# Where the first dense layer's gate is computed: m(2t - m) with three passes on VectorE in place of max, add and min over VectorE and GpSimd

## The chip, the cores and the metric

The kernel runs on one core of a Trainium2 chip. A core has five engines with queues of their own: TensorE (PE, matrix products and transposes), VectorE (DVE), ScalarE (ACT), GpSimd (POOL) and SyncE (SP, which here issues the DMAs). Each works through its queue in order; between engines, semaphores say when an input is there. The metric is the time of one execution on the device, in microseconds (us), lower being better.

## The reference

An attention over 4 batches, 8 heads, 1152 positions and 64 columns, whose queries are averaged in pairs (576 queries remain), then two dense layers over the resulting 2304 rows of 512 columns. The gate that the change concerns is `g`:

```python
h = x @ w_in                                   # 2304 x 2048
g = np.where(h >= 1, h, np.where(h <= -1, 0.0, (h + 1) ** 2 / 4))
x = g @ w_out                                  # 2304 x 512
h = np.maximum(np.maximum(x @ w1, x @ w2), x @ w3)
out = h @ w_o2
```

With t = relu(h/2 + 1/2), the gate is 0 where t is 0, t squared where t is up to 1, and 2t - 1 above. Both the old and the new formula give that.

## The kernel before

The attention runs in 48 units: batch b, a block i of 192 queries, and a pair p of heads. Each unit computes three blocks of scores (line 352, 128 x 1152, "sc"). For each block DVE takes the row maximum (line 366, "st"), ScalarE turns it into a bias (367) and takes the exponentials (368, "pf"). For two of three blocks, in batches 1 to 3, ScalarE then makes a half-precision copy (421), DVE subtracts it to get the rest (422, "hl"), and a DMA transposes both. The third block is transposed by TensorE (404), copied by ScalarE (410) and its rest is taken by DVE (411). The product with the values is line 440 ("av"), scaled by DVE in line 453 ("xf") and, every fourth unit, split into two half-precision parts (245 on GpSimd, 246 on DVE). The same pair of lines splits queries, keys and values. Queries come by DMA and are added in pairs by GpSimd in line 321 ("qn"). The next batch's keys and values are prepared in four units around a change of batch.

The first dense layer follows the attention by six units: from then on each unit also holds two tiles of the "up" product (line 506, 48 products of 192 columns) and one block of the "down" product (line 532). An up tile is 128 x 384 and goes through lines 511 to 517: ScalarE makes t (511, tile "t2", "t" in the profile), three operations make the gate in place with a second tile "rl", GpSimd makes its half-precision part (515) and DVE the rest (517). Both are inputs of line 532. There are 96 such tiles. Twelve come after the last unit, in a tail in which the second layer's weights are prepared as well (lines 155 to 161, 147, 148, 664 to 675). One of the four weight blocks there is split on GpSimd, in lines 672 and 673. The second layer (lines 752 to 785) comes last.

The order on TensorE is written out by hand for the attention (`ORDER`); on the other engines, and in the tail on TensorE too, a scheduler puts the instructions in order when the program is built, from its own estimate of their durations. A change of a few operations can so move others. "t2" and "rl" have two buffers each.

Of the kernel before, what the change touches and what calls it, by code (L numbers as in the profile page):

```python
# [12 lines left out]
ALU = mybir.AluOpType  # L13
# [38 lines left out]
def body(ctx: ExitStack, tc: tile.TileContext, q, k, v, w_in, w_out, w1, w2, w3, w_o2, out):  # L52
    nc = tc.nc
# [416 lines left out]
    def scales(b):  # L470
        hu = small.tile([P, 1], F32, tag="hu", name=f"hu{b}")
        hh = small.tile([P, 1], F32, tag="hh", name=f"hh{b}")
        nc.vector.tensor_scalar(out=hu, in0=U_in[:, 1:2], scalar1=Uv[b][:, NPAIR:NPAIR + 1],
                                scalar2=None, op0=ALU.mult)
        nc.vector.tensor_scalar(out=hh, in0=Uv[b][:, NPAIR + 1:NPAIR + 2], scalar1=0.5, scalar2=None, op0=ALU.mult)

        gd = small.tile([P, 1], F32, tag="dgd", name=f"dgd{b}")
        gs = small.tile([P, 1], F32, tag="dgs", name=f"dgs{b}")
        nc.vector.tensor_scalar(out=gd, in0=hu, scalar1=2.0 ** 31, scalar2=1.0, op0=ALU.mult, op1=ALU.max)
        nc.vector.tensor_scalar(out=gd, in0=gd, scalar1=2.0 ** -15, scalar2=None, op0=ALU.mult)  # L480
        nc.vector.reciprocal(out=gs, in_=gd)
        dst[b] = hh, gd, gs
# [3 lines left out]
    def acc(x, name):  # L486
        ps, tag = room[x]
        return ps.tile([P, 512], F32, tag=tag, name=name)

    def up_steps(b, i):  # L490

        if i == 0:
            scales(b)
        hh, gd, gs = dst[b]
        x = xh.pop((b, i))
        g = gp.tile([P, 2, NF, NB], F16, tag="g", name=f"g{b}_{i}")
        gt[b, i] = g
        for f2 in range(NF // 2):
            key = f"{b}_{i}_{f2}"
            fs = slice(2 * f2, 2 * f2 + 2)  # L500
            ph = acc("h", "ph" + key)[:, :2 * NB].rearrange("p (a n) -> p a n", a=2)
            for a in range(2):
                ff = 2 * f2 + a
                for kt in range(KD):
                    for e, (wi, xi) in enumerate(((0, 0), (0, 1), (1, 0))):
                        nc.tensor.matmul(ph[:, a], win[:, wi, kt, ff * P:(ff + 1) * P], x[:, xi, kt],  # L506
                                         start=(kt == 0 and e == 0), stop=(kt == KD - 1 and e == 2))

            t2 = room["t2"].tile([P, 2, NB], F32, tag="t2", bufs=room["n"], name=f"t2_{key}")
            rl = room["t2"].tile([P, 2, NB], F32, tag="rl", bufs=room["n"], name=f"rl_{key}")  # L510
            nc.scalar.activation(out=t2, in_=ph, func=AF.Relu, scale=hh, bias=0.5)
            nc.vector.tensor_scalar(out=rl, in0=t2, scalar1=1.0, scalar2=-1.0, op0=ALU.max, op1=ALU.add)  # L512
            nc.gpsimd.tensor_tensor(out=rl, in0=t2, in1=rl, op=ALU.add)  # L513
            nc.vector.scalar_tensor_tensor(out=t2, in0=t2, scalar=1.0, in1=rl, op0=ALU.min, op1=ALU.mult)  # L514
            nc.gpsimd.tensor_scalar(out=g[:, 0, fs, :], in0=t2, scalar1=gs, scalar2=1.0,  # L515
                                    op0=ALU.mult, op1=ALU.mult)
            nc.vector.scalar_tensor_tensor(out=g[:, 1, fs, :], in0=t2, scalar=gs, in1=g[:, 0, fs, :],  # L517
                                           op0=ALU.mult, op1=ALU.subtract)
            yield
# [20 lines left out]
    def dense_steps(units):  # L540

        down = iter(())
        for b, i in units:
            for k, _ in enumerate(up_steps(b, i)):
                yield
                if k % 2 == 1:
                    next(down, None)
                    yield
                    yield
            down = down_steps(b, i)  # L550
        for _ in down:
            yield
            yield
# [299 lines left out]
```

## Time and profile before

| | before |
|---|---|
| median of 2 runs | 1233.24 us (1231.83 to 1234.66) |
| the profiled execution | 1239.84 us, span on the core 1237.9 us |
| PE busy | 1077.9 us (87%) |
| DVE busy | 857.5 us (69%), 1454 instructions |
| ACT busy | 696.8 us (56%) |
| POOL busy | 302.9 us (24%), 306 instructions |
| mean granted TensorE clock | 0.958 of full speed |

Line numbers are those of the kernel before. Times within the trace count from the start of the span. In a timeline a row says when an instruction began, how long it took, and in brackets how long its engine was idle before and what ended that. Instructions of one engine overlap by a little at their edges. The shares in the table are means over stages that have different limits, so stages and waits are read one by one.

### The profile page before, as it was taken

The numbers are of one execution on the slowest core, as the hardware profiler recorded it, in microseconds if no ns is written. First come the engines' busy times: TensorE is split into PE (matmuls) and PEld (weight loads), VectorE is DVE, ScalarE is ACT, GpSimd is POOL, SyncE is SP. The second block draws the span as 40 slices with busy tenths as digits, with TensorE's granted clock in tenths as the row PEclk, the third lists the DMA queues.
The fourth block names the chain that finished last, engine by engine and source line by source line (L and its number), as shares of the span: only waits on it lengthen the run. The fifth ranks groups of instructions, "written<-read, shape, count | busy, mean of one in ns | idle before, by whom it ended". The sixth has DMA issues, their size and how long they took to land.

```text
span 1237.9 us, 26735 instructions
## 1 busy us (share of the span) xinstructions
PE 1077.9 (87%) x11058; PEld 881.2 (71%) x11058; DVE 857.5 (69%) x1454; ACT 696.8 (56%) x1241; POOL 302.9 (24%) x306
## 2 busy tenths in 40 slices
PE   0456788899999987999988899998697999999998
PEld 0334567677788876888877788887696876767774
DVE  3988765657888888988888988886988652322220
ACT  3868676656667777667776677766453411122111
POOL 1310012323222344322234422221643020100000
PEclk9867889999999999999999999999899999999999
DMA  9963211446766688965588766547433220000001
GB/s 289 267 199 106 90 27 26 84 87 155 129 113 120 109 172 170 167 110 110 110 158 177 146 105 107 97 88 157 160 96 117 90 67 18 10 27 18 17 18 43
DMA packets 273753, 134.90 MB, mean 109 GB/s; under 512 B 229088, under 2 KB 256736, under 8 KB 272608
## 3 DMA queue, kind: packets, MB, share of 16 engines
q1 hardware_dynamic: 273632, 133.20, 48.5%
q8 instruction: 86, 1.41, 0.5%
q14 instruction: 35, 0.29, 0.1%
HBM read 62.39 MB, written 9.44 MB: 58 GB/s over the span
## 4 chain that ended last, share of the span: by engine, by line
PE 41%; DVE 17%; issue 7%; DMA 7%; ACT 6%; POOL 4%; SPq 2%; ACTq 0%; POOLq 0%; DVEq 0%
PE p L752 17%; PE po L769 5%; PE ph L506 5%; PE py L532 4%; DVE st L366 4%; DMA qn<-in_q_dram 3%; PE sc L352 3%; PE tr L404 3%; PE av L440 2%; DVE g L517 2%; DVE hl L422 2%; DVE t L514 2%; ACT pf L368 1%; POOL g L515 1%; ACT hl L421 1%
## 5 line engine op out<-in xcount | busy, mean ns | idle before, releaser
L352 PE MATMUL sc<-kst,qst 128*64 128x512 f16 (+3 forms) x1152 | 178.2, 347 | 62.6 <-DMA qst<-qpre 21.1
L532 PE MATMUL py<-g,wou 128*128 128x192 f16 x2304 | 201.1, 248 | 22.4 <-POOL g L515 7.8
L752 PE MATMUL p<-yh,wm 128*128 128x288 f16 x1728 | 216.0, 287 | 3.7 <-ACT py L536 2.7
L532 PEld LDWEIGHTS <-wou 128*128 128x128 f16 x2304 | 191.3, 99 | 31.8 <-issue 31.4
L506 PE MATMUL ph<-xh,win 128*128 128x192 f16 x2304 | 203.2, 249 | 4.9 <-ACT py L536 2.6
L366 DVE TENSOR_REDUCE st<-sc 128x1 f32<-128x1152 f32 x144 | 194.1, 1348 | 18.0 <-PE sc L352 17.8
L752 PEld LDWEIGHTS <-wm 128*128 128x128 f16 x1728 | 169.6, 98 | 49.6 <-issue 4.4
L506 PEld LDWEIGHTS <-win 128*128 128x128 f16 x2304 | 195.1, 99 | 7.5 <-issue 5.7
L368 ACT ACTIVATE pf<-sc,st,esc 128x1152 f32<-128x1152 f32 x144 | 188.7, 1311 | 4.5
L352 PEld LDWEIGHTS <-qst 128*64 128x64 f16 (+1 forms) x1152 | 85.6, 109 | 124.3 <-issue 56.9
L513 POOL TENSOR_TENSOR rl<-t,rl 128x384 f32<-128x384 f32 x96 | 103.7, 1083 | 185.3 <-DVE rl L512 185.3
L404 PE MATMUL tr<-ident,pf 128*128 128x128 f32 x648 | 98.9, 306 | 26.3 <-ACT pf L368 17.4
L422 DVE TENSOR_TENSOR hl<-pf,hl 128x1152 f16<-128x1152 f32 x72 | 104.3, 1449 | 22.7 <-ACT hl L421 22.6
L404 PEld LDWEIGHTS tr<-ident,pf 128*128 128x128 f32 x648 | 83.5, 161 | 40.9 <-ACT pf L368 24.8
L367 ACT ACTIVATE st<-st,esc 128x1 f32<-128x1 f32 x144 | 41.6, 289 | 119.0 <-DVE st L366 118.8
L760 ACT ACTIVATE h<-mx 128x288 f16<-128x288 f32 x48 | 21.2, 442 | 133.3 <-DVE mx L758 133.3
L757 DVE TENSOR_TENSOR mx<-p,mx 128x288 f32<-128x288 f32 x48 | 21.9, 456 | 106.3 <-PE p L752 105.7
L515 POOL TENSOR_SCALAR g<-t,dgs 128x384 f16<-128x384 f32 x96 | 70.7, 738 | 97.0 <-DVE t L514 91.4
L440 PE MATMUL av<-pt,vhl 128*64 128x192 f16 x1944 | 87.1, 247 | 2.7 <-DMA pt<-hl 2.7
L440 PEld LDWEIGHTS <-vhl 128*64 128x64 f16 x1944 | 79.3, 110 | 12.4 <-issue 8.5
L517 DVE SCALAR_TENSOR_TENSOR g<-t,dgs,g 128x384 f16<-128x384 f32 x96 | 74.2, 781 | 16.4 <-POOL g L515 16.2
L421 ACT ACTIVATE hl<-pf 128x1152 f16<-128x1152 f32 x72 | 83.4, 1159 | 0.9
(169 smaller groups left out, 1339.0 us busy)
## 6 DMA issues: line engine op xcount, KB each, us to landing
kn<-in_k_dram SPq DMA_DIRECT2D x16, 576.0 KB, 4.6
vn<-in_v_dram SPq DMA_DIRECT2D x16, 576.0 KB, 5.0
raw_m<-in_moe_w_dram SPq DMA_DIRECT2D x12, 768.0 KB, 5.1
raw_in<-in_moe_w_in_dram SPq DMA_DIRECT2D x8, 1024.0 KB, 5.4
qn<-in_q_dram SPq DMA_DIRECT2D x24, 256.0 KB, 4.0
raw_ou<-in_moe_w_out_dram SPq DMA_DIRECT2D x10, 512.0 KB, 4.6
qst<-qst SPq DMA_DIRECT2D x48, 96.0 KB, 2.2
y_d<-ys SPq DMA_DIRECT2D x48, 96.0 KB, 2.0
```

Of the source, the lines that this page charges most:

```text
L352: nc.tensor.matmul(sc[m0:m1, n0:n1], qst[b, i, p][who][:, var, m0:m1], ks[:, h, n0:n1], start=(var == 0), stop=(var == 1))
L366: nc.vector.tensor_reduce(out=m, in_=sc, axis=AX.X, op=ALU.max, negate=True)
L368: nc.scalar.activation(out=pf, in_=sc, func=AF.Exp, bias=nb, scale=e, accum_out=sums[b, i, p][:, who:who + 1])
L404: nc.tensor.transpose(tr[:, c * P:(c + 1) * P], pf[:, c * P:(c + 1) * P], ident)
L421: nc.scalar.activation(out=hl[:, 0], in_=pf, func=AF.Copy)
L422: nc.vector.tensor_tensor(out=hl[:, 1], in0=pf, in1=hl[:, 0], op=ALU.subtract)
L440: nc.tensor.matmul(acc[64 * h:64 * h + 64], vhl[b, p][:, vi, h, c, :], pt[:, h, pi * KT + c, :], start=(c == 0 and e == 0), stop=(c == KT ...
L506: nc.tensor.matmul(ph[:, a], win[:, wi, kt, ff * P:(ff + 1) * P], x[:, xi, kt], start=(kt == 0 and e == 0), stop=(kt == KD - 1 and e == 2))
L513: nc.gpsimd.tensor_tensor(out=rl, in0=t2, in1=rl, op=ALU.add)
L517: nc.vector.scalar_tensor_tensor(out=g[:, 1, fs, :], in0=t2, scalar=gs, in1=g[:, 0, fs, :], op0=ALU.mult, op1=ALU.subtract)
L532: nc.tensor.matmul(py, wou[:, ff // 2, wi, ff % 2, m * P:(m + 1) * P], g[:, gi, ff, :], start=(ff == 0 and e == 0), stop=(ff == NF - 1 and ...
L752: nc.tensor.matmul(ph[:, :NB2], wm[:, wi, i, kt, ff * P:(ff + 1) * P], yh[:, yi, kt, n0:n0 + NB2], start=(kt == 0 and e == 0), stop=(kt == ...
```

## The change

Three lines of the gate are replaced. Before: rl = max(t, 1) - 1 on DVE, rl = t + rl on GpSimd, t = min(t, 1) * rl on DVE. Now: rl = min(t, 1), t = 2t - rl, t = t * rl, all on DVE. Lines 511, 515 and 517 stay.

```diff
-            nc.vector.tensor_scalar(out=rl, in0=t2, scalar1=1.0, scalar2=-1.0, op0=ALU.max, op1=ALU.add)
-            nc.gpsimd.tensor_tensor(out=rl, in0=t2, in1=rl, op=ALU.add)
-            nc.vector.scalar_tensor_tensor(out=t2, in0=t2, scalar=1.0, in1=rl, op0=ALU.min, op1=ALU.mult)
+            nc.vector.tensor_scalar(out=rl, in0=t2, scalar1=1.0, scalar2=None, op0=ALU.min)
+            nc.vector.scalar_tensor_tensor(out=t2, in0=t2, scalar=2.0, in1=rl, op0=ALU.mult, op1=ALU.subtract)
+            nc.vector.tensor_tensor(out=t2, in0=t2, in1=rl, op=ALU.mult)
```

The first place is DVE's queue in a steady unit (batch 1, block 2 of the attention around it; the tiles are the first two of batch 2's first dense block; minus is before, plus is now, the rest stands in both).

```order
 L512 TENSOR_SCALAR rl_0_0_7278<-t_2_0_0_7277 128x384
+L513 SCALAR_TENSOR_TENSOR t_2_0_0_7277<-t_2_0_0_7277,rl_0_0_7278 128x384
 L422 TENSOR_TENSOR hl_1_2_0_7340<-pf_1_2_0_7226,hl_1_2_0_7340 128x1152
-L514 SCALAR_TENSOR_TENSOR t_2_0_0_7277<-t_2_0_0_7277,rl_0_0_7278 128x384
+L514 TENSOR_TENSOR t_2_0_0_7277<-t_2_0_0_7277,rl_0_0_7278 128x384
 L512 TENSOR_SCALAR rl_0_1_7311<-t_2_0_1_7310 128x384
 L366 TENSOR_REDUCE st_1_2_1_7334<-sc_1_2_1_7327 128x1
+L513 SCALAR_TENSOR_TENSOR t_2_0_1_7310<-t_2_0_1_7310,rl_0_1_7311 128x384
 L517 SCALAR_TENSOR_TENSOR g_0_7251<-t_2_0_0_7277,dgs_7247,g_0_7251 128x384
-L514 SCALAR_TENSOR_TENSOR t_2_0_1_7310<-t_2_0_1_7310,rl_0_1_7311 128x384
 L453 SCALAR_TENSOR_TENSOR xf_1_7121<-av_1_1_7344,Uv_6075,R_1_1_7318 128x192
+L514 TENSOR_TENSOR t_2_0_1_7310<-t_2_0_1_7310,rl_0_1_7311 128x384
```

The first tile's new line 513 stands ahead of line 422, the second tile's ahead of line 517, and the second tile's line 514 moves behind line 453.

The second place is DVE's queue in a unit in which, before, both first-stage operations of the two tiles were done before either of the last ones (batch 1's third dense block, tiles 2 and 3).

```order
 L366 TENSOR_REDUCE st_0_3_1_6531<-sc_0_3_1_6524 128x1
-L514 SCALAR_TENSOR_TENSOR t_1_2_2_6474<-t_1_2_2_6474,rl_2_2_6475 128x384
-L514 SCALAR_TENSOR_TENSOR t_1_2_3_6507<-t_1_2_3_6507,rl_2_3_6508 128x384
+L513 SCALAR_TENSOR_TENSOR t_1_2_3_6507<-t_1_2_3_6507,rl_2_3_6508 128x384
+L517 SCALAR_TENSOR_TENSOR g_2_6197<-t_1_2_2_6474,dgs_4005,g_2_6197 128x384
 L453 SCALAR_TENSOR_TENSOR xf_0_6074<-av_0_2_6541,Uv_6075,R_0_2_6515 128x192
-L517 SCALAR_TENSOR_TENSOR g_2_6197<-t_1_2_2_6474,dgs_4005,g_2_6197 128x384
+L514 TENSOR_TENSOR t_1_2_3_6507<-t_1_2_3_6507,rl_2_3_6508 128x384
+L366 TENSOR_REDUCE st_0_3_2_6611<-sc_0_3_2_6598 128x1
 L517 SCALAR_TENSOR_TENSOR g_2_6197<-t_1_2_3_6507,dgs_4005,g_2_6197 128x384
-L366 TENSOR_REDUCE st_0_3_2_6611<-sc_0_3_2_6598 128x1
```

The third maximum (line 366, block 2) moves ahead of the second tile's line 517.

The third place is GpSimd's queue in the tail (tiles 6 and 7 of batch 3's second dense block, around the weight block that GpSimd splits).

```order
-L513 TENSOR_TENSOR rl_1_6_12281<-t_3_1_6_12280,rl_1_6_12281 128x384
-L513 TENSOR_TENSOR rl_1_7_12321<-t_3_1_7_12320,rl_1_7_12321 128x384
 L672 TENSOR_SCALAR st_m_12154<-st_m_12154,s_m 128x2304
+L673 TENSOR_TENSOR wm<-st_m_12154,wm 128x3x768
 L515 TENSOR_SCALAR g_1_11532<-t_3_1_6_12280,dgs_10489 128x384
-L673 TENSOR_TENSOR wm<-st_m_12154,wm 128x3x768
 L515 TENSOR_SCALAR g_1_11532<-t_3_1_7_12320,dgs_10489 128x384
```

Line 513 is gone, and line 673 moves ahead of the first line 515.

## Rows read from the trace of the kernel before

**Rows 1.** Stages: window, length, busy time and instructions of each engine, TensorE clock, DMA.
```profile
475.00:550.00 75.00, 67.01 (x807) 58.97 (x808) 64.75 (x113) 51.75 (x96) 27.89 (x27) 0.98 0.77 148
...
775.00:850.00 75.00, 75.00 (x983) 66.49 (x985) 62.34 (x88) 52.15 (x96) 17.71 (x23) 1.00 0.53 93
...
905.00:945.00 40.00, 35.83 (x427) 35.03 (x425) 35.92 (x58) 17.52 (x27) 16.03 (x15) 1.00 0.35 114
```

**Rows 2.** Waits, 174 to 860 us: waiter, awaited, us in total, times, longest.
```profile
PE tr L404 <- ACT pf L368: 16.6, 17, 2.3
PE py L532 <- DVE xf L453: 7.6, 8, 1.8
...
DVE g L517 <- POOL g L515: 14.5, 19, 3.1
```

**Rows 3.** Single lines: duration in ns, minimum/median/maximum; last row from the page, with mean.
```profile
L512 DVE TENSOR_SCALAR rl<-t x96: 341/354/1184, 173.9 to 937.6; 128x384 f32<-128x384 f32 x96
L514 DVE SCALAR_TENSOR_TENSOR t<-t,rl x96: 541/546/1340, 177.4 to 939.7; 128x384 f32<-128x384 f32 x96
L517 DVE SCALAR_TENSOR_TENSOR g<-t,dgs,g x96: 601/613/4896, 180.9 to 941.1; 128x384 f16<-128x384 f32 x96
L422 DVE TENSOR_TENSOR hl<-pf,hl x72: 1342/1353/1937, 288.1 to 853.4; 128x1152 f16<-128x1152 f32 x72
...
L517 DVE SCALAR_TENSOR_TENSOR g<-t,dgs,g 128x384 f16<-128x384 f32 x96 | 74.2, 781 | 16.4 <-POOL g L515 16.2
```

**Rows 4.** Timeline of DVE, a steady unit: start, us, instruction, idle before.
```profile
548.72 0.36 DVE L512 TENSOR_SCALAR rl<-t 128x384 f32<-128x384 f32 x1 [0.73 <-ACT t L511]
549.78 1.60 DVE L422 TENSOR_TENSOR hl<-pf,hl 128x1152 f16<-128x1152 f32 x1 [0.69 <-ACT hl L421]
551.30 0.55 DVE L514 SCALAR_TENSOR_TENSOR t<-t,rl 128x384 f32<-128x384 f32 x1
551.77 0.35 DVE L512 TENSOR_SCALAR rl<-t 128x384 f32<-128x384 f32 x1
...
554.66 1.34 DVE L366 TENSOR_REDUCE st<-sc 128x1 f32<-128x1152 f32 x1
```

**Rows 5.** Timeline of GpSimd, that unit and the next.
```profile
549.17 0.99 POOL L513 TENSOR_TENSOR rl<-t,rl 128x384 f32<-128x384 f32 x1 [8.95 <-DVE rl L512]
...
567.98 0.99 POOL L321 TENSOR_TENSOR qn<-qn 128x384 f32<-128x384 f32 x1 [3.31 <-DMA qn<-in_q_dram]
568.95 0.58 POOL L515 TENSOR_SCALAR g<-t,dgs 128x384 f16<-128x384 f32 x1
569.50 0.99 POOL L513 TENSOR_TENSOR rl<-t,rl 128x384 f32<-128x384 f32 x1
```

**Rows 6.** Timelines of DVE and TensorE, the same two units.
```profile
569.57 1.35 DVE L517 SCALAR_TENSOR_TENSOR g<-t,dgs,g 128x384 f16<-128x384 f32 x1 [1.68 <-POOL g L515]
...
571.63 1.35 DVE L366 TENSOR_REDUCE st<-sc 128x1 f32<-128x1152 f32 x1
...
552.77 1.14 PE L352 MATMUL sc<-kst,qst 128*64 128x512 f16 x12
...
567.28 1.14 PE L352 MATMUL sc<-kst,qst 128*64 128x512 f16 x12
...
574.79 1.20 PE L404 MATMUL tr<-ident,pf 128*128 128x128 f32 x9 [1.33 <-ACT pf L368]
```

**Rows 7.** Timeline of GpSimd in the tail.
```profile
884.00 3.33 POOL L513 TENSOR_TENSOR rl<-t,rl 128x384 f32<-128x384 f32 x2 [3.69 <-DVE rl L512]
887.30 3.28 POOL L672 TENSOR_SCALAR st_m<-st_m,s_m 128x2304 f32<-128x2304 f32 x1
...
892.20 5.24 POOL L673 TENSOR_TENSOR wm<-st_m,wm 128x2304 f16<-128x2304 f32 x1
897.42 0.88 POOL L515 TENSOR_SCALAR g<-t,dgs 128x384 f16<-128x384 f32 x1
```

**Rows 8.** Timeline of TensorE in the tail.
```profile
897.90 0.96 PE L532 MATMUL py<-g,wou 128*128 128x192 f16 x5 [5.30 <-DVE g L517]
```

## The prediction

> **What bounds the kernel now.** I read the stage view first. From 775 to 850 us TensorE is busy for the whole 75 us while VectorE (DVE) has 62.34: there TensorE alone sets the pace [rows 1]. From 475 to 550 us it is 67.01 of 75 against DVE's 64.75, so neither fills the stage; they wait for each other. In the tail, 905 to 945 us, DVE has 35.92 of 40 and TensorE 35.83, again with waits on both sides. The changed lines run only from 173.9 to 941.1 us [rows 3], so what the change can move is TensorE's waiting between these.
>
> The waits come second. Between 174 and 860 us TensorE waits 16.6 us, in 17 pieces, for the exponentials (line 368) before it transposes, and 7.6 us in 8 pieces for line 453 [rows 2]. DVE itself waits 14.5 us, 19 times, at line 517 for GpSimd's line 515 [rows 2]. The exponential waits for DVE's maximum (line 366), so a DVE held at 517 is late with the maximum, and TensorE then stands.
>
> Third, one steady unit on DVE [rows 4]. Line 512 runs at 548.72 for 0.36 us, and then DVE stands 0.69 us until ScalarE has the half-precision copy that line 422 needs. Line 422 takes 1.60 us, against its minimum of 1342 ns [rows 3], with GpSimd's line 513 running beside it from 549.17 for 0.99 us [rows 5].
>
> **The change, step by step.** There are 96 tiles: two in each of 42 attention units, and twelve in the dense tail.
>
> *GpSimd loses line 513*: 96 executions of about 0.99 us [rows 5], some 95 us off its queue. GpSimd was mostly idle before it, so that alone is worth nothing on the path; what counts is what it held up.
>
> *Line 512* keeps its shape and loses its second operation. I leave its 354 ns [rows 3]. The dropped operation can have cost between nothing and all of it; a minimum of 341 ns at 384 columns, below one operation of line 422 per column, leaves little, so I take nothing.
>
> *New line 513* (2t - m, two tensor inputs and a scalar) is of the form of old line 514: median 546 ns [rows 3]. In the queue such an instruction moves the next one by 0.47 us (551.30 to 551.77) [rows 4]. *New line 514* is a plain product of the same two tiles. The trace has no such operation at this size. Above lies the three-operand form, 541 ns; below, a third of line 422's 1342 ns for three times the columns, 447 ns, or, if it ran at line 512's rate, 354 ns [rows 3]. I take 546, since it is nearest to line 514 in shape and in its two fp32 inputs; the lower end would be worth 96 x 0.19 = 18 us of DVE, in the range with a third of that on the path. The Trainium skill ("VectorE: DVE Perf Modes", section "Why `tensor_tensor` can't do 2×_2P or 4×") says a two-tensor fp32 operation cannot double its rate, because the second tensor takes the second read port; line 422's minimum agrees, and by it the sum stays as it is.
>
> So DVE gains 96 x 0.47 = 45 us of queue. Against that stands the stretching that disappears. Line 517 has a mean of 781 ns and a minimum of 601 [rows 3]; times 96 that is 17 us. Line 422 lost 0.26 us at 549.78. Line 513 is the longest thing GpSimd runs beside them, so I put about 25 us of stretch on it over all lines (estimated), and net DVE work at +20 us.
>
> *Where those go, stage by stage.*
>
> Steady units. The diff puts new 513 right behind 512, ahead of 422. 549.08 + 0.55 = 549.63 lies inside the 0.69 us wait that ends at 549.78: hidden, and if the copy came earlier it would cost 0.47. Line 422 then has no line 513 beside it, and new 514 starts 0.26 us earlier than old 514. The second tile's 513 adds 0.47 us ahead of 517, so the third maximum moves by about +0.2 us. In the stage 775 to 850 us TensorE never waits for it. Change: 0.
>
> Units in which GpSimd first waits for a q load. At 567.98 it gets to line 321, then 515 at 568.95, then 513 at 569.50 [rows 5]. DVE stands 1.68 us for 515, and its line 517 takes 1.35 us beside that 513 instead of 0.60; the third maximum starts at 571.63 and TensorE waits 1.33 us at 574.79 [rows 6]. Afterwards new 513 of the second tile fits into the 1.68 us, and 517 is 0.75 us shorter; the maximum comes some 0.7 us earlier and TensorE's wait falls to about 0.6. Where the q load was ahead of both 513s, the diff also moves the third maximum ahead of the second 517. Of the 17 waits (mean 0.98 us) I count ten with 0.5 us each: -5 us. Bounds: 0 if q's landing alone sets it, -8 if half of the 16.6 us goes.
>
> Units that also split the next batch's keys and values (12 of them). DVE has next to no idle time there, so each pays up to 2 x 0.47 = 0.94 us; each gets back the stretch, up to 0.75 on line 517 and 0.3 on 422. Line 453, for which TensorE waits 7.6 us, moves behind new 513 and 422 in some of them and comes later. I take 0, between 12 x -0.5 and 12 x +0.6 (-6 to +7).
>
> Units from 174 to 300 us. DVE has spare time, and the new order ends the wait between 513 and 514, but puts 0.47 us a tile ahead of the maximum in the first unit: -1, an estimate; its twelve tiles bound it at 12 x 0.47 = +5 and, if one wait of GpSimd's 0.99 us goes in four units, at -4.
>
> Tail. At 884.00 GpSimd takes two line 513s, to 887.33, which keeps line 672 waiting; then 672, 515, 673 and at 897.42 the last 515 [rows 7]. TensorE waits 5.30 us for the tile behind it [rows 8]. Without the 513s, 672 can start when ScalarE has read its input, which I put at 2 of these 3.33 us, and the diff has 673 directly behind it and both 515s after: the last 515, with less beside it, ends near 895.5 instead of 898.3, -3 us; the first comes later than now, but the last decides. From there to 945 us eight tiles put 8 x 0.47 = 4 us on a DVE that is 90% busy, and about 5 us of stretch goes. Tail: -4 (-8 to +4).
>
> Sum: -5 + 0 - 1 - 4 = -10 us on the profiled execution of 1239.84 us (span 1237.9): 1230. That execution lies 6.6 us above the median of the two timed runs, 1233.24, so on the median's scale the forecast is 1233.24 - 10, rounded to 1224 us.
>
> **Rivals.**
>
> *A wash.* The DVE work that is added eats what GpSimd's release gives: TensorE's waits stay at 16.6 + 7.6 us and only change names. For it speaks that DVE is at 64.75 of 75; against it that the first of each pair of 513s lies in a wait that exists. Within 4 us: about 1233 us.
>
> *DVE becomes the bound (slower).* Place: the 32 units before 700 us and the tail. If new 513 didn't fit ahead of 422, and the third maximum came late by 0.94 us in each of them, TensorE would wait that much at line 404: +30 us, 12 x 0.47 = +6 in the tail, less the 5 above, +31: 1264 us. From which lateness on it decides, the rows say. In the stalled unit the scores end at 567.28 + 1.14 = 568.42, the maximum starts at 571.63 and TensorE loses 1.33 us, so a start at 570.30, 1.9 us after the scores, would have cost nothing [rows 6]. In the steady unit they end at 553.91 and the maximum starts at 554.66, 0.75 us after [rows 4, 6]; my +0.2 makes it 0.95, so a further 0.95 us would be needed. A milder form, +3 to +20, is likelier than the full one.
>
> *Contention comes back.* The two new DVE instructions read two SBUF tiles each; if GpSimd's 515 ran beside them, each could stretch as line 517 did, by 0.75 us, 96 times, a third of it on the path: +24 us, 1247 us after the gain. Against it: 515 starts when new 514 ends, and in the new order 512 and the maximum are what follows, so 515's 0.58 us are over before the next new 513. The Trainium skill ("GPSIMD Engine Reference", section "8. Key points") names just this sharing, GpSimd against DVE operations with two SBUF inputs; the rows of line 517 agree that it happens.
>
> *The whole of it.* All of the 17 waits go and the tail gains its 8 us: -16.6 - 8 - 4 = -29 us, 1205 us. For it: every such wait hangs on the same queue. Against: q's landing stays.
>
> **How the numbers follow.** Forecast, a gain of 4 to 20 us: 0.56. A wash: 0.22. Slower by 4 to 24 us, with contention in it: 0.11. DVE the bound, over 2%: 0.04. The whole gain, over 2%: 0.07. Two per cent, 24.7 us, is about what a measurement of this kernel can tell from no change. So faster 0.07, same 0.89, slower 0.04. The lower bounds add up to -8 - 6 - 4 - 8 = -26 us, the upper ones to +16. I cut to -22 and +5, 1211 to 1238 us, which leaves out the whole gain (0.07) and most of the two slower cases (0.13 of 0.15). The likeliest case's own range is 1213 to 1229.
>
> **What would show it.** Right: line 422 at 1.35 us in steady units; 517 with a mean near 0.65 us; DVE's busy time up by 15 to 30 us; the wait of line 404 for 368 down to 8 to 13 us; the last 515 behind line 672 in the tail under 10.5 us after its start; a stage like that at 775 to 850 us in which TensorE still never waits. Wrong: line 404's wait above 20 us; new 513 or 514 above 0.65 us in the mean; line 422's idle time in front gone and its start later; that last 515 later.

## The result, and the profile after

The changed kernel takes 1218.00 us (1216.47 to 1219.53, two runs) where the kernel before takes 1233.24: a ratio of 0.9887, 95% interval 0.9857 to 0.9917 (the quotient of the two medians, 0.9876, lies inside it). Run again with more executions on another chip it was 1220.37 against 1237.59 us, ratio 0.9857 (0.9836 to 0.9878). (The kernel before has medians from 1233.2 to 1239.4 us on the chips used here, so each ratio is to runs beside it.) So the gain is 14 to 18 us; 10 were forecast, and both medians lie in the range of 1211 to 1238 and in the likeliest case's own 1213 to 1229. Against the bound of 2% this is no change that counts as faster, as forecast; but the intervals, 0.2 to 0.3% to either side, leave out 1, so it is a gain and not noise.

The page of the changed kernel: busy time of each engine, then three lines of the gate and line 422 (count, busy, mean ns, then idle time before and what ended it).

```profile
PE 1078.7 (89%) x11058; PEld 884.2 (73%) x11058; DVE 872.9 (72%) x1550; ACT 697.5 (57%) x1241; POOL 212.5 (17%) x210
...
L515 POOL TENSOR_SCALAR g<-t,dgs 128x384 f16<-128x384 f32 x96 | 82.6, 861 | 319.7 <-DVE t L514 315.1
...
L422 DVE TENSOR_TENSOR hl<-pf,hl 128x1152 f16<-128x1152 f32 x72 | 98.5, 1368 | 5.8 <-ACT hl L421 3.2
...
L517 DVE SCALAR_TENSOR_TENSOR g<-t,dgs,g 128x384 f16<-128x384 f32 x96 | 61.1, 637 | 23.7 <-POOL g L515 23.7
```

VectorE is busy for 15.4 us more than the 857.5 before, GpSimd 90.4 less than its 302.9. Line 517's mean fell from 781 ns [rows 3] to 637. Line 422 waited 22.6 us for ScalarE's copy before; now 3.2: the new line 513 stands in that place.

Single lines of the changed kernel (minimum, median, maximum in ns), then its waits from 174 to 860 us.

```profile
L513 DVE SCALAR_TENSOR_TENSOR t<-t,rl x96: 541/552/1462, 176.0 to 918.8; 128x384 f32<-128x384 f32 x96
L514 DVE TENSOR_TENSOR t<-t,rl x96: 540/550/1356, 178.1 to 919.4; 128x384 f32<-128x384 f32 x96
```

```profile
DVE g L517 <- POOL g L515: 16.8, 17, 3.3
...
PE tr L404 <- ACT pf L368: 8.7, 8, 2.2
PE sc L352 <- ACT R L388: 8.6, 5, 3.2
...
PE py L532 <- DVE xf L453: 6.6, 6, 2.1
```

The product costs what the three-operand form costs, 550 ns. TensorE's wait for the exponentials has halved, from 16.6 us in 17 pieces [rows 2] to 8.7 in 8; VectorE's wait for GpSimd at line 517 has not fallen.

For the comparison of stages I cut each trace at the start of the first maximum (line 366) of a unit. Lengths in us:

| trace | units 6 to 12 | 13 to 38 | 39 to 46 | 47 to the end |
|---|---|---|---|---|
| before (the one predicted from) | 132.8 | 424.4 | 116.1 | 396.4 |
| before, second trace | 126.0 | 424.1 | 116.1 | 397.0 |
| changed | 122.8 | 418.5 | 116.2 | 392.0 |
| changed, second trace | 124.9 | 420.3 | 116.3 | 389.1 |

Units 39 to 46, the steady ones, did not move. The others all gave something, and the first stage of the trace that I predicted from was 6.8 us longer than in the second.

### The profile page after: what moved, and what is told of

It reads as the page before. It is cut to its first block, busy times and chain, and to the rows that moved or that the text cites. A ratio compares the mean times of both kernels' runs of the same rounds, so it can differ in the third digit from the quotient of the medians.

```text
span 1217.8 us, 26735 instructions
## 1 busy us (share of the span) xinstructions
PE 1078.7 (89%) x11058; PEld 884.2 (73%) x11058; DVE 872.9 (72%) x1550; ACT 697.5 (57%) x1241; POOL 212.5 (17%) x210
## 4 chain that ended last, share of the span: by engine, by line
PE 54%; DVE 17%; DMA 8%; ACT 8%; issue 6%; POOL 5%; SPq 1%; ACTq 0%; POOLq 0%; DVEq 0%
PE p L752 17%; PE py L532 9%; PE ph L506 7%; PE sc L352 6%; PE po L769 5%; PE av L440 4%; PE tr L404 3%; DMA kn<-in_k_dram 3%; DVE st L366 3%; DMA qn<-in_q_dram 2%; ACT pf L368 2%; POOL g L515 2%; DVE g L517 2%; DVE hl L422 1%; DVE kpre L246 1%
## 5 line engine op out<-in xcount | busy, mean ns | idle before, releaser
L532 PE MATMUL py<-g,wou 128*128 128x192 f16 x2304 | 205.8, 251 | 18.9 <-POOL g L515 10.7
L532 PEld LDWEIGHTS <-wou 128*128 128x128 f16 x2304 | 195.9, 100 | 21.1 <-issue 20.1
L366 DVE TENSOR_REDUCE st<-sc 128x1 f32<-128x1152 f32 x144 | 194.5, 1350 | 15.7 <-PE sc L352 15.4
L515 POOL TENSOR_SCALAR g<-t,dgs 128x384 f16<-128x384 f32 x96 | 82.6, 861 | 319.7 <-DVE t L514 315.1
L404 PEld LDWEIGHTS tr<-ident,pf 128*128 128x128 f32 x648 | 82.4, 159 | 32.4 <-ACT pf L368 16.4
L422 DVE TENSOR_TENSOR hl<-pf,hl 128x1152 f16<-128x1152 f32 x72 | 98.5, 1368 | 5.8 <-ACT hl L421 3.2
L517 DVE SCALAR_TENSOR_TENSOR g<-t,dgs,g 128x384 f16<-128x384 f32 x96 | 61.1, 637 | 23.7 <-POOL g L515 23.7
L769 PE MATMUL po<-wo,h 128*128 128x512 f16 x288 | 64.3, 379 | 0.0
```

The lines of the kernel that those rows point to most:

```text
L366: nc.vector.tensor_reduce(out=m, in_=sc, axis=AX.X, op=ALU.max, negate=True)
L404: nc.tensor.transpose(tr[:, c * P:(c + 1) * P], pf[:, c * P:(c + 1) * P], ident)
L422: nc.vector.tensor_tensor(out=hl[:, 1], in0=pf, in1=hl[:, 0], op=ALU.subtract)
L532: nc.tensor.matmul(py, wou[:, ff // 2, wi, ff % 2, m * P:(m + 1) * P], g[:, gi, ff, :], start=(ff == 0 and e == 0), stop=(ff == NF - 1 and ...
L769: nc.tensor.matmul(po, h2t[b][:, hi, ff, t * P:(t + 1) * P], wo[:, wi, ff, :], start=(ff == 0 and e == 0), stop=(ff == NF2 - 1 and e == 2))
```

## The experiments

The theory: GpSimd's add held up what stood behind it on GpSimd and stretched VectorE's instructions beside it; the 45 us that VectorE takes over fit into waits that it had. The rivals: the form of the three passes counts; the scheduler's new order counts; the early gain is chance; VectorE is the bound now.

**The changed kernel again** (no edit).

> The changed kernel once more, unedited, for a second trace and a narrower interval. Theory (the gain comes from GpSimd's queue: no line 513 in it, and the value split ahead of the pair add of a q that is not due): the unit in which GpSimd waited 6.05 us for q before (26.1 us long before, 21.1 after) is again under 22 us, ratio 0.985 to 0.990. Rival (the early 7 us were a matter of when one load happened to land): that unit comes out anywhere between 21 and 26 us, and the ratio near 0.993.

Measured: 1220.37 us, ratio 0.9857 (0.9836 to 0.9878). The unit that took 26.1 us before and 21.1 after takes 23.8 here. The ratio went the theory's way, the unit did not come out under 22: it varies with the execution.

**The old formula with its add on VectorE.**

```diff
-            nc.gpsimd.tensor_tensor(out=rl, in0=t2, in1=rl, op=ALU.add)
+            nc.vector.tensor_tensor(out=rl, in0=t2, in1=rl, op=ALU.add)
```

> The old formula, min(t,1) * (t + max(t,1) - 1), with nothing changed but the engine of its add: VectorE instead of GpSimd. GpSimd and SyncE then have the same order as in the changed kernel, VectorE the same number of passes. Theory (only the engine of the add counts): 1218 us, within 3, and VectorE's busy time within 3 us of 872.9. Rival (the form of the three passes counts, since line 512 loses an operation and the last pass has no scalar): 3 to 8 us above the changed kernel.

Measured: 1218.71 us, ratio 0.9843 (0.9819 to 0.9866), VectorE busy 874.1 us. The new algebra does nothing that can be measured; the engine of one of the passes is the whole change. All queues have the changed kernel's order in this run, so it does not tell the engine from the order that the scheduler makes of it.

**A GpSimd add of the same size that nobody waits for.**

```diff
+            nc.gpsimd.tensor_tensor(out=sk, in0=rl, in1=rl, op=ALU.add)
```

> The changed kernel, plus a GpSimd add of the size of the old line 513 for every tile, into a tile that nothing reads, so that GpSimd's load is back and VectorE does not wait for it. Theory (the gain is GpSimd's freed queue and the stretch that goes with it): line 422's mean back above 1.42 us, line 517's above 0.72, and 1228 to 1240 us, since the 45 us of VectorE stay. Rival (what helped is that VectorE no longer waits for GpSimd inside the gate, and the order): 1217 to 1222 us.

Measured: 1245.82 us, 25.5 over the changed kernel run beside it and over the 1240 that I had allowed, ratio to before 1.0065 (1.0046 to 1.0084). Its page (the idle add stands under line 512) and two of its waits from 174 to 860 us:

```profile
L512 POOL TENSOR_TENSOR sk<-rl 128x384 f32<-128x384 f32 x96 | 108.3, 1129 | 183.2 <-DVE rl L512 182.0
...
L422 DVE TENSOR_TENSOR hl<-pf,hl 128x1152 f16<-128x1152 f32 x72 | 108.3, 1504 | 2.6
...
L517 DVE SCALAR_TENSOR_TENSOR g<-t,dgs,g 128x384 f16<-128x384 f32 x96 | 66.2, 692 | 26.6 <-POOL g L515 26.6
```

```profile
PE tr L404 <- ACT pf L368: 15.2, 15, 2.2
PE py L532 <- DVE xf L453: 14.9, 8, 2.8
```

Line 422 is at 1504 ns in the mean (1368 in the changed kernel, 1449 before), TensorE's wait for the exponentials is back at 15.2 us, and VectorE is busy for 904.6 us, 31.7 more than without the add, with nothing in the gate waiting for it. (Line 517 stayed under the 720 ns expected.) So such an add costs this kernel 25 us without anybody waiting for it. The order of all queues is the changed kernel's up to the tail, so the part of the 25 us that lies in units 13 to 38 (433.9 us against 418.5 and 420.3) owes nothing to the scheduler; in the tail it moved instructions. Read as steps, the change is then VectorE's 45 us for a cost of some 8 us (1237.59 to 1245.82), and the load taken off GpSimd for a gain of 25.5. The two prices hold for this order of steps only: the idle add runs beside the new passes, and stretches line 422 more than the old add did.

**One more VectorE pass for nothing.**

```diff
+            nc.vector.tensor_tensor(out=sk, in0=t2, in1=rl, op=ALU.add)
```

> The changed kernel plus one more VectorE pass for every tile (t + m into a tile that nothing reads), 96 x 0.47 = 45 us of VectorE's queue for nothing: the price of VectorE time by itself, the same amount that the change added. Theory (the first 45 us went into waits that VectorE had; this second lot finds them mostly filled, and is paid in the units that load q, keys and values and in the tail): 8 to 20 us slower than the changed kernel, 1227 to 1240. Rival (VectorE still has room): within 4 us. Rival (VectorE has been the bound since the change): 35 to 45 us slower.

Measured: 1257.89 us, ratio 1.0162 (1.0143 to 1.0181); against 0.9857 that is 1.0309, some 38 us over the changed kernel. I had expected 8 to 20; the rival, VectorE at its bound, has the right number for this second lot. Its reason is not shown: VectorE is busy for 922.6 us of the 1257.9, and the scheduler put the idle pass ahead of line 513 and moved others, so that VectorE's order differs from the changed kernel's in all 42 units with tiles. The 38 us are the price of the pass in that order. One steady unit of it, TensorE and VectorE:

```profile
807.39 1.14 PE L352 MATMUL sc<-kst,qst 128*64 128x512 f16 x12
...
813.92 1.20 PE L404 MATMUL tr<-ident,pf 128*128 128x128 f32 x9 [0.34 <-ACT pf L368]
```

```profile
810.76 1.34 DVE L366 TENSOR_REDUCE st<-sc 128x1 f32<-128x1152 f32 x1
```

The scores end at 807.39 + 1.14 = 808.53, the maximum starts 2.23 us later, and TensorE waits 0.34 us: by that row 1.89 would have cost nothing. The prediction put that point at 1.9 us. (The unit is 15.06 us long and 14.51 in the changed kernel; by that the point lies nearer 1.7.)

**The new gate in a part of the tiles only.** One condition; the other tiles keep the old gate.

```diff
+            new = 8 * (b * NBL + i) + f2 < 14           # early
+            new = 14 <= 8 * (b * NBL + i) + f2 < 84     # middle
+            new = 8 * (b * NBL + i) + f2 >= 84          # tail
```

> The new gate in the first 14 of the 96 tiles alone, those of the first seven units with tiles (about 168 to 300 us); the old gate behind. Theory (some 7 us of the gain come from this stretch): 4 to 9 us under the kernel before. My prediction's term: 1 us, within the error. Rival (the early gain in the traces is chance): 0 to 2 us.

Measured: 1227.66 against 1233.77 us, ratio 0.9957 (0.9941 to 0.9973): 5.3 us (3.3 to 7.3). Its units 6 to 12 take 122.2 us.

> The new gate in the 70 tiles between the first 14 and the last 12 alone (units 13 to 47). Prediction's terms for these units: steady 0, units that load q 5 us less, units that split keys and values 0, so 5 us under the kernel before (bounds 14 under to 7 over). If the three parts add up to the whole (0.986 of 1237 us is 17 us under, 0.9957 and 0.9955 for the early part and the tail are 5.3 and 5.6), this part comes out 6 us under. Rival (the parts share their gain, since each moves the later stages' loads): 0 to 3 us.

Measured: 1230.37 against 1239.36 us, ratio 0.9928 (0.9901 to 0.9954): 8.9 us (5.7 to 12.3). In its trace the units 13 to 38 take 106.3 + 164.8 + 147.7 = 418.8 us, 5.5 less than before.

> The new gate in the last 12 of the 96 tiles alone, those of the dense tail. Prediction's term: 4 us under the kernel before (bounds 8 under to 4 over); line 672 starts right after line 671 and not behind two line 513s. Rival (the tail's VectorE, 90% busy, eats it): 0 to 2 us over.

Measured: 1227.60 against 1233.77 us, ratio 0.9955 (0.9938 to 0.9972): 5.6 us (3.5 to 7.6). From unit 47 to the end it takes 390.3 us, 6 to 7 less than before.

The three parts add up to 19.8 us, the whole is 17.7 (15.1 to 20.3) in the run with more executions: they add, within what can be measured.

**Order alone: the value split ahead of the pair add.** In the first trace of the kernel before, GpSimd's pair add (line 321) waited 6.05 us for a q that is needed many units later, with a value split behind it; in the changed kernel the scheduler put the split first. The edit does that for the one place, in the kernel before: a one-column write on GpSimd (1.47 us in its trace) that the load then overwrites ties the load to the split.

```diff
+        if b == 1 and i == 2 and p == 0:
+            nc.gpsimd.tensor_scalar(out=qn[:, 0, 0, 0:1], in0=vhl[b, 1][:, 0, 0, 0, 0:1],
+                                    scalar1=1.0, scalar2=None, op0=ALU.mult)
```

> The kernel before, with one edit of order: a one-column write on GpSimd makes the pair add of one q (batch 1, i = 2, p = 0) and its loads follow the value split of batch 1, p = 1. Theory (the early part of the gain is that split no longer queued behind an add that waits for its load): the 26.1 us unit falls to 22 or less, VectorE's 4.4 us wait for the split there goes, and the time falls by 4 to 7 us to 1226 to 1229. Rival (the early gain comes from line 513 being gone): no change, 1232 to 1235.

Measured: 1238.16 us (12 executions), ratio 1.0012 (0.9988 to 1.0037), yet the profiled one took 1231.45 with units 6 to 12 in 123.9 us. So both kernels were run once more, for a second trace.

> The kernel with the value split ahead of the pair add once more, for a second trace, since its profiled execution (1231.45 us) was the fastest of its twelve while their median was no better than that of before. If that execution was the odd one, the stretch of seven units, 123.9 us long in its trace, comes out at 129 to 133 us now; if the edit works and something later pays it back, 124 again and the later units longer by 6.

Measured: 1228.88 us (one execution), units 6 to 12 in 123.8 us.

> The kernel before once more, unedited, for a second trace. From it: how much of the 132.8 us between the start of the unit at 168.1 us and that at 300.9 us comes back. Theory (the changed kernels' 123 to 125 us there are the change's doing): 130 to 135 us again. Rival (that stretch is a matter of the execution, since the granted clock fell to 0.63 from 240 us on only in the first trace): 124 to 127 us.

Measured: 1232.06 us (one execution), units 6 to 12 in 126.0 us. What had made them 132.8 shows in two stages of the kernel before, first trace and second trace (window, length, busy times of TensorE, its weight loads, VectorE, ScalarE and GpSimd, then TensorE's clock, DMA share, GB/s):

```profile
240.00:250.00 10.00, 6.99 (x34) 4.70 (x34) 6.48 (x9) 5.78 (x12) 3.37 (x4) 0.63 0.29 75
```

```profile
240.00:250.00 10.00, 9.86 (x109) 8.43 (x109) 6.81 (x17) 5.92 (x11) 3.20 (x4) 1.00 0.20 53
```

In the first trace TensorE had stood 2.98 us for the exponentials at 241.74; it then ran at a granted clock of 0.63 in the mean, between its two levels of 1.2 and 2.4 GHz. In the second it stood 1.15 us at the same place and kept 2.4 GHz. That unit took 26.07 us in the one and 20.84 in the other, although the pair add waited 7.36 us in the second; so the wait that the order edit takes away is not what made the unit long. The trace I predicted from held an accident of some 5 us there, and a smaller one in unit 6 (18.52 against 16.44). Neither belongs to the kernel before alone: in the changed kernel's second trace the same unit took 23.8 us, at a clock of 0.85 from 240 to 250 us, and unit 6 took 18.52 in the run with the new gate in the early tiles. The order edit shows 2 us in two traces, while its times allow 1.5 us of gain at most; what it is worth stays open.

**GpSimd's last part of the gate on ScalarE.**

```diff
-            nc.gpsimd.tensor_scalar(out=g[:, 0, fs, :], in0=t2, scalar1=gs, scalar2=1.0, ...)
+            nc.scalar.activation(out=g[:, 0, fs, :], in_=t2, func=AF.Copy, scale=gs)
```

> The changed kernel with line 515 (the half-precision part of g) on ScalarE instead of GpSimd, so that the gate uses GpSimd no more. Theory (what is left of the waits at line 517, 16.8 us between 174 and 860, comes from line 515 standing behind GpSimd's wait for q): those go, ScalarE takes on 96 x 0.57 = 55 us (line 511's time) where it is 57% busy, and the time falls by 3 to 10 us to 1208 to 1215. Rival (the exponentials of line 368, for which TensorE waits, now stand behind it): 5 to 20 us slower than the changed kernel.

Measured: 1218.29 us, ratio 0.9844 (0.9827 to 0.9862): the same as the changed kernel, so neither theory nor rival. Line 517's wait is gone, but for 2.2 of its 23.7 us:

```profile
L517 DVE SCALAR_TENSOR_TENSOR g<-t,dgs,g 128x384 f16<-128x384 f32 x96 | 61.7, 648 | 2.2 <-ACT g L515 2.1
```

A wait of VectorE went and nothing was gained; ScalarE, for whose exponentials TensorE waits, is busy for 48.2 us more (697.5 to 745.7). TensorE's waits for ScalarE are longer by it: from 174 to 860 us 12.5 us for line 388 and 11.7 for line 368, where the changed kernel has 8.6 and 8.7.

**The pair add of q on VectorE.**

```diff
-        nc.gpsimd.tensor_tensor(out=qp, in0=qn[:, :, 0, :], in1=qn[:, :, 1, :], op=ALU.add)
+        nc.vector.tensor_tensor(out=qp, in0=qn[:, :, 0, :], in1=qn[:, :, 1, :], op=ALU.add)
```

> The changed kernel with the pair add of q (line 321, 24 of them, the one GpSimd instruction that waits for a load) on VectorE. Theory: GpSimd no longer stands in front of line 515 and the splits; waits at line 517 fall under 10 us; VectorE takes 24 x 0.47 = 11 us: 0 to 6 us faster than the changed kernel. Rival: now VectorE stands for q's load with the maxima behind it, 5 to 30 us slower; it decides if VectorE's waits for q come to more than 10 us.

Measured: 1231.04 us, ratio 0.9945 (0.9924 to 0.9965), 0.9945 / 0.9857 or some 11 us over the changed kernel. Its waits from 174 to 860 us:

```profile
DVE qn L321 <- DMA qn<-in_q_dram: 20.0, 10, 3.4
```

The rival's point, 10 us of waiting for q on VectorE, is passed. The theory's own sign came too: line 517 waits only 2.8 us for GpSimd, where 10 were allowed, and it did not help. The same 24 adds waited 77.6 us for q on GpSimd in the changed kernel; 20.0 us of it on VectorE cost 11 us.

No version ran faster than the changed kernel by more than the intervals.

## Why the prediction was right, and where its terms were not

The direction and the place of the gain were right: TensorE waits less for the exponentials, and the gain lies outside the steady units. The sum was too small, -10 against 14 to 18 us, and its parts were partly right by luck, as the stages show. (1233.24 - 10 is 1223.2, so the forecast should have read 1223.)

**Steady units, 0: right.** One of them in the changed kernel, VectorE:

```profile
771.93 0.36 DVE L512 TENSOR_SCALAR rl<-t 128x384 f32<-128x384 f32 x1 [0.73 <-ACT t L511]
772.33 0.56 DVE L513 SCALAR_TENSOR_TENSOR t<-t,rl 128x384 f32<-128x384 f32 x1
772.98 1.36 DVE L422 TENSOR_TENSOR hl<-pf,hl 128x1152 f16<-128x1152 f32 x1
...
778.05 1.35 DVE L366 TENSOR_REDUCE st<-sc 128x1 f32<-128x1152 f32 x1
```

The new 513 lies where VectorE stood 0.69 us before [rows 4], line 422 takes 1.36 us instead of 1.60, and the third maximum starts 0.94 us after the scores (they end at 775.97 + 1.14 = 777.11), where 0.95 was forecast. And TensorE (first of the engines in the stage's row) never waits:

```profile
775.97 1.14 PE L352 MATMUL sc<-kst,qst 128*64 128x512 f16 x12
```

```profile
755.00:805.00 50.00, 49.97 (x653) 44.26 (x652) 43.77 (x65) 35.93 (x66) 5.35 (x8) 1.00 0.62 101
```

What I did not say is how little is left: in the kernel with one more pass the maximum of such a unit starts 2.2 us after the scores, 1.3 later than here, and the eight units take 123.2 us against 116.2.

**Units with q loads, -5: right mechanism, too small.** The eight of them took 131.0 and 130.2 us in the two traces before and 122.3 and 122.6 after: -8. The unit shown before, now:

```profile
554.79 1.00 POOL L321 TENSOR_TENSOR qn<-qn 128x384 f32<-128x384 f32 x1 [6.10 <-DVE t L513]
555.77 0.59 POOL L515 TENSOR_SCALAR g<-t,dgs 128x384 f16<-128x384 f32 x1
```

```profile
556.39 0.62 DVE L517 SCALAR_TENSOR_TENSOR g<-t,dgs,g 128x384 f16<-128x384 f32 x1 [1.64 <-POOL g L515]
...
557.72 1.35 DVE L366 TENSOR_REDUCE st<-sc 128x1 f32<-128x1152 f32 x1
```

```profile
553.91 1.14 PE L352 MATMUL sc<-kst,qst 128*64 128x512 f16 x12
...
560.88 1.20 PE L404 MATMUL tr<-ident,pf 128*128 128x128 f32 x9 [0.79 <-ACT pf L368]
```

Line 517 takes 0.62 us instead of 1.35, with no 513 behind GpSimd's 515 [rows 5, 6]; the maximum starts 2.67 us after the scores instead of 3.21, and TensorE waits 0.79 instead of 1.33 (forecast 0.6). In units like this my half microsecond holds. It fell short where the third maximum went ahead of the second line 517, which I had seen in the order and not priced: units 15, 19, 27 and 31 are 1.1, 1.4, 2.6 and 1.1 us shorter, and TensorE waits no more there. Much of that is the order: with the idle add put back and VectorE's order as in the changed kernel, the four take 61.1 us, where they took 64.8 before and 58.5 after. So 3.7 of their 6.2 us stay with the add running; what they owe to the order and what to VectorE not waiting for the add was not tried apart.

**Units that split keys and values, 0: some 2 us slower.** Units 13, 14, 22 to 26 and 34 to 38 took 205.8 and 206.1 us before and 208.6 and 210.2 after. Over all traces with the old gate in these units (six, 205.8 to 209.5) and with the gate's three passes on VectorE and nothing added (four, 208.6 to 210.2) the means are 207.3 and 209.1. Four units (14, 23, 26 and 35) lose 1.7 to 2.4 us, two a little, and the other six win up to 1.9. Unit 23, from 445 us on, VectorE, GpSimd, ScalarE and TensorE:

```profile
450.13 1.46 DVE L513 SCALAR_TENSOR_TENSOR t<-t,rl 128x384 f32<-128x384 f32 x1
```

```profile
449.81 1.37 POOL L245 TENSOR_SCALAR vhl<-vn,sb 128x1152 f16<-128x1152 f32 x1 [3.48 <-DVE Uv L451]
```

```profile
453.99 1.16 ACT L266 ACTIVATE kpre<-kn 128x1152 bf16<-128x1152 f32 x1 [3.43 <-DMA kn<-in_k_dram]
...
456.32 0.22 ACT L388 ACTIVATE R<-tr 64x64 f32<-64x64 f32 x1
```

```profile
456.59 1.17 PE L352 MATMUL sc<-kst,qst 128*64 128x512 f16 x12 [3.19 <-ACT R L388]
```

ScalarE's line 266 in that unit before:

```profile
463.49 1.16 ACT L266 ACTIVATE kpre<-kn 128x1152 bf16<-128x1152 f32 x1 [1.22 <-DMA kn<-in_k_dram]
```

The new pass is stretched by GpSimd's split beside it to 1.46 us, as the contention rival had it, though by a split and not by line 515. But the 3.19 us that TensorE waits here do not come from VectorE: line 388 stands behind line 266 in ScalarE's queue, and that one waits 3.43 us for a load of keys, where it waited 1.22 before and TensorE 0.95. It is so in the other traces too: 3.0 to 3.4 us in four with the new gate here, 1.2 in four with the old. Why that load comes later in its unit was not tried apart. My step had looked at VectorE alone. With the q units this makes -5 over units 13 to 38 in the traces (424.4 and 424.1 to 418.5 and 420.3), which is what I had, by two errors that cancel; the times say 8.9 (5.7 to 12.3), and the means over all such traces, 425.3 and 419.2, say 6.

**Units from 174 to 300 us, -1: mis-sized.** The times say -5.3, beyond my bound of -4. In the traces it is -8 to -10 against the first of before, and -1.1 to -3.2 against the second, which kept its clock. What is the change's doing lies in unit 12 (20.0 us in both traces before, 16.2 and 16.7 after, 16.4 with the new gate in the early tiles alone). Its row of TensorE before:

```profile
283.96 4.12 PE L506 MATMUL ph<-xh,win 128*128 128x192 f16 x48 [1.91 <-ACT py L536]
```

The wait follows ScalarE's line 266, which waits for a key load, 4.70 us before and 3.30 after; and VectorE's low part of the keys, 1.42 us, moved behind the first maximum of unit 13. My step looked at the gate's own lines and left out that transfers and splits come earlier too. Two more traces have the old gate in the early tiles (those with the new gate in the middle and in the tail alone, 129.6 and 126.5 us for units 6 to 12) and two more the new passes (old formula on VectorE 123.5, early tiles alone 122.2): the means of four are 128.7 and 123.4, 5.4 us apart, as the times say, and unit 12 takes 19.8 to 20.0 in the one four and 16.2 to 16.7 in the other. The low clock in unit 10 is in two of the four with the old gate and in one with the new, so how much of the rest is chance, four traces of each can't settle. (That stage has fourteen tiles, not twelve, so the upper bound should have been +7.)

**Tail, -4: right in size (-5.6), wrong in its steps.** GpSimd and TensorE in the changed kernel:

```profile
868.44 6.94 POOL L672 TENSOR_SCALAR st_m<-st_m,s_m 128x2304 f32<-128x2304 f32 x1 [4.81 <-ACT wm L671]
875.46 4.54 POOL L673 TENSOR_TENSOR wm<-st_m,wm 128x2304 f16<-128x2304 f32 x1
879.98 1.15 POOL L515 TENSOR_SCALAR g<-t,dgs 128x384 f16<-128x384 f32 x2
```

```profile
880.62 0.32 PE L532 MATMUL py<-g,wou 128*128 128x192 f16 x1 [7.00 <-POOL g L515]
910.70 13.36 PE L532 MATMUL py<-g,wou 128*128 128x192 f16 x129 [3.67 <-POOL g L515]
927.58 1.81 PE L532 MATMUL py<-g,wou 128*128 128x192 f16 x20 [1.37 <-DVE g L517]
930.43 19.83 PE L752 MATMUL p<-yh,wm 128*128 128x288 f16 x158 [0.68 <-DVE yh L725]
```

TensorE in the kernel before, its first wait there and the later ones (its second, 5.30 us, is in [rows 8]; two short ones, 0.23 and 0.56, are left out):

```profile
892.28 0.32 PE L532 MATMUL py<-g,wou 128*128 128x192 f16 x1 [5.37 <-POOL g L515]
...
927.27 2.31 PE L532 MATMUL py<-g,wou 128*128 128x192 f16 x26 [0.94 <-POOL g L515]
930.48 3.05 PE L532 MATMUL py<-g,wou 128*128 128x192 f16 x35 [0.90 <-DVE g L517]
935.06 1.15 PE L532 MATMUL py<-g,wou 128*128 128x192 f16 x12 [1.54 <-POOL g L515]
...
948.08 0.77 PE L752 MATMUL p<-yh,wm 128*128 128x288 f16 x5 [2.71 <-ACT py L536]
949.84 15.40 PE L752 MATMUL p<-yh,wm 128*128 128x288 f16 x114 [0.98 <-DVE yh L725]
```

Line 672 starts at once when line 671 is done, as I said, but takes 6.94 us instead of 3.28 [rows 7], with VectorE busy beside it without a gap until 873.31 us; the last 515 ends 12.7 us after its start, where I allowed 10.5 (11.0 before). TensorE's first wait there is longer (7.00 us, 5.37 before), the second shorter (3.67, 5.30 before): 10.67 us together in either kernel, so the 3 us that I had put on line 672 did not come. The gain stands behind these: from there on the changed kernel has two more waits before its next stage runs (1.37 and 0.68, 2.05 us), where the kernel before had seven, the longest 2.71, 7.86 us together. The second traces say the same, 9.67 and 7.33 us before, 10.91 and 2.06 after. What shortened the later waits was not tried apart; the order on TensorE differs there as well.

**VectorE's net work, +20: right** (15.4; forecast 15 to 30). With 45 us added, some 30 of stretch went, where I had 25. But my sum gave back only 10 us of TensorE's time for it, and the idle add showed that such an add alone, with its stretch, costs 25 us on the path.

## What to carry to other kernels

An add on an idle engine is not free: here some 100 us on a GpSimd busy for a quarter of the time cost 25 us through what it stretched and what stood behind it, and 45 us more on a VectorE busy for 70% cost some 8. But the room that took them was small: the next 45 us, in the order that the scheduler then made, cost 38, so ask of each steady stage how late its deciding instruction may still come. Take a second trace before pricing a stage from one: a spell of low clock made one unit 5 us longer in one execution than in the next. Follow a wait to its end before naming its cause: the longest one of unit 23 was a load that ScalarE waited for, not the stretched pass beside it.

## What the runs showed of the hardware that I had not expected

In the rows below VectorE and GpSimd shut each other out for whole instructions, in both directions. VectorE in the kernel before, beside line 673 (892.20 to 897.44 us [rows 7]):

```profile
892.95 4.90 DVE L517 SCALAR_TENSOR_TENSOR g<-t,dgs,g 128x384 f16<-128x384 f32 x1
```

A pass of 0.6 us ends only after GpSimd's 5.24 us have ended. The reverse in the changed kernel, GpSimd and then VectorE's first and last row beside it:

```profile
905.76 4.89 POOL L515 TENSOR_SCALAR g<-t,dgs 128x384 f16<-128x384 f32 x1 [3.08 <-DVE t L514]
```

```profile
905.59 0.35 DVE L512 TENSOR_SCALAR rl<-t 128x384 f32<-128x384 f32 x1
...
907.67 2.60 DVE L148 SCALAR_TENSOR_TENSOR wm<-st_m,s_m,wm 128x2304 f16<-128x2304 f32 x1
```

A GpSimd pass of 0.58 us stood until VectorE, without a gap from 905.59 on, had ended line 148 at 910.27. Line 672 shows it as well: in the changed kernel it ends 2.07 us after VectorE's run without a gap, and it took 2.18 us in all in the run with the idle add, where VectorE stood idle for most of it. The Trainium skill ("SBUF — State Buffer", section "SBUF: two separate sides") describes a lock on the pair of ports that the two share: of a GpSimd instruction and a VectorE one that has two SBUF inputs or runs in a two-port mode, whichever starts first holds it to its end and the other is blocked. Both rows agree; the second adds that a chain of VectorE instructions keeps GpSimd out for its whole length. By that rule the price of a GpSimd instruction is set by what it meets, not by how long it takes alone.
